# Loads of v behind the spread of the batch before, first v spread by VectorE, new planner costs: a sparse attention with a maxout layer on one core

## The chip, the core and the metric

The kernel runs on one core of a Trainium2 chip. Its engines are TensorE (PE; its weight loads are shown as PEld), VectorE (DVE), ScalarE (ACT), GpSimd (POOL) and SyncE (SP), which here only issues DMA transfers. Sixteen DMA engines move the data of the core. The metric is the device time of one execution in microseconds; lower is better. A time of a kernel is the median of its runs.

## The reference

```python
# q, k, v: (4, 8, 768, 64) float32; block = 32, window = 16, nb = 24, scale = 1/8
k_sum = k.reshape(B, H, nb, block, D).max(axis=3)
v_sum = v.reshape(B, H, nb, block, D).mean(axis=3)
scores_l = scale * q @ k.T                      # kept where |i - j| < window
scores_s = scale * einsum('bhsd,bhnd->bhsn', q, k_sum) + log(block)
a = softmax(concat[where(mask_l, scores_l, -1e9), scores_s])
attn = a @ concat[v, v_sum]                     # (B, H, S, D)
x = attn.transpose(0, 2, 1, 3).reshape(3072, 512)
h1, h2 = x @ w1, x @ w2                         # w1, w2: 512 x 1024
out = maximum(h1, h2) @ w_out                   # w_out: 1024 x 512
```

Each query sees its 31 nearest keys and 24 block summaries. The result then goes through a layer that takes the larger of two products, and a last product.

## The kernel before

**Work.** Four batches of eight heads, handled as four head pairs (hp). For a head pair, k and q are loaded, cast to bf16, turned by TensorE, and placed in kx and qx; kx gets the 24 block maxima beside the keys of each of 12 tiles of 64 queries. Scores of four tiles at a time (three groups a head pair) go through exp on ScalarE into pb, and are masked. The product with v ("values", line 448) takes pb as weights and a row block of vx; VectorE divides by the sums, TensorE turns the result into xt. The maxout part is written as x w1 w_out + relu(x (w2 - w1)) w_out: "hidden" (line 548, wd = w2 - w1), relu on ScalarE, and "out", which starts with w1o = w1 w_out (line 562) and adds the rest (line 569). It runs over 256 rows at a time, three groups a batch.

**The v tile.** vx holds, for each of 12 query tiles, 128 rows: 96 rows of v (64 and 32, the neighbourhood of the tile) and 32 rows (64 to 95) with the 24 block means. It is filled in steps: `load_v` loads v in two halves (line 277, 768 KB each, vf), GpSimd casts them into vb (line 328), five transfers from SBUF to SBUF put vb's rows in place (line 294: two of 64 rows by 6 tiles, three pieces of 32 rows that are together as large as one of these), TensorE computes the means from vb (line 302), VectorE copies them into tile 0 (line 308), and a last transfer copies tile 0's means to the other 11 tiles (line 316, "vx<-vx"). All of a batch's value products read that tile, so they need the last transfer. There is one vb and there are two vx; batches 0, 1, 2, 3 use vx_95, vx_95, vx_96, vx_95 in the listings below, and the turned w1 uses vx_96 in between.

**Order.** The program is written out by a planner. Every task has an engine, a guessed duration and a priority. `Plan.run` steps through time: for each engine that is free it takes the first task in order of priority whose inputs are done and whose buffers are free, and assumes that it takes the guessed time. What comes out is one fixed list of instructions per engine; on the chip each engine works through its list in order and waits where it must. So a changed guess moves instructions on all engines. SP is planned with four transfers at a time in flight, one after the other:

```python
                if e == "SP":
                    busy[e] = now + self.ISSUE
                    t.done = max(sent[-1], now + 0.4) + t.us
```

All transfers of the program, loads, spreads and stores, are issued by SP in one list. A store (line 580) waits on SP for ScalarE's copy of its tile, and all that stands behind it on SP waits too.

Of the kernel before, what the change touches and what calls it, by code (L numbers as in the profile page):

```python
# [16 lines left out]
ACT = mybir.ActivationFunctionType  # L17
# [41 lines left out]
class Task:  # L59
    done = 1e9  # L60


class Plan:
# [7 lines left out]

    def op(self, engine, us, fn, read=(), write=(), change=(), touch=(), prio=0.0, label=""):
        t = Task()
        t.engine, t.us, t.fn, t.label = engine, us, fn, label
        t.prio = (prio, len(self.tasks))
        t.new = [*write, *change]
# [5 lines left out]
        self.tasks.append(t)  # L82

    def ready(self, t, now):
        if any(d.done + self.LAG[d.engine] > now for d in t.deps):
            return False
        need = [b for b in dict.fromkeys(t.new) if b.slot is None]
        slots = [b.ring.find(b, now) for b in need]
        if None in slots:
            return False  # L90
        for b, s in zip(need, slots):
            b.take(s)
        return True
# [33 lines left out]
def kernel(  # L127
# [14 lines left out]
    nc = tc.nc  # L142
# [11 lines left out]
    op = plan.op  # L154
# [31 lines left out]
    w1t = Buf(vxr)  # L186
# [20 lines left out]
    def fixed_parts():  # L207
# [57 lines left out]
    def load_kq(b, hp, prio):  # L265
        for n, src in enumerate((k, q)):
# [3 lines left out]
               write=[f], prio=prio, label=f"load {'kq'[n]}{b}{hp}")  # L270

    def load_v(b, prio, engines):

        vb = Buf(vbr)
        for n in range(2):
            f = Buf(vfr)
            op("SP", 3.45, lambda f=f, n=n: nc.sync.dma_start(
                out=f.ap[:].rearrange("p h m d -> p (h m) d"),
                in_=v[b, 4 * n:4 * n + 4].rearrange("h (m r) d -> r (h m) d", r=128)),
               write=[f], prio=prio, label=f"load v{b}{n}")  # L280
            copy(engines[n], 1536, lambda f=f, n=n: (
                vb.ap[:, :, 4 * n:4 * n + 4, 0:D].rearrange("p m h d -> p h m d"), f.ap[:]),
                 read=[f, amean_in], write=[vb], prio=prio + 1, label=f"cast v{b}{n}")
# [4 lines left out]
        for lo, hi, tiles_, part, ms, us in (
                (0, 64, slice(0, NT, 2), 0, slice(0, NM), 1.3),
                (0, 64, slice(1, NT, 2), 64, slice(0, NM), 1.3),  # L290
                (96, 128, slice(0, NT, 2), 64, slice(0, NM), 0.65),
                (96, 128, slice(1, NT - 1, 2), 0, slice(1, NM), 0.6),
                (96, 128, slice(NT - 1, NT), 0, slice(0, 1), 0.2)):
            op("SP", us, lambda lo=lo, hi=hi, tiles_=tiles_, part=part, ms=ms: nc.sync.dma_start(  # L294
                out=rows(vx[b].ap[lo:hi, tiles_]),
                in_=rows(vb.ap[part:part + hi - lo, ms])),
               read=[vb], write=[vx[b]], prio=prio + 2, label=f"spread v{b}")
# [13 lines left out]

        def spread_means():
            o, i = rows(vx[b].ap[s, 1:NT]), rows(vx[b].ap[s, 0:1])
            i = i.to_broadcast([32, NT - 1, H * VW])
            if engines[2] == "SP":
                nc.sync.dma_start(out=o, in_=i)
            else:
                nc.vector.tensor_copy(out=o, in_=i)

        op(engines[2], 1.2 if engines[2] == "SP" else 1.6, spread_means, read=[mean],  # L320
           write=[vx[b]], prio=prio + 2, label=f"spread means {b}")

    RATE = {"DVE": 0.00068, "ACT": 0.00102, "POOL": 0.00102}

# [7 lines left out]
    def prep(b, hp, prio, k_on, q_on):  # L332
# [28 lines left out]
        op("DVE", 0.9, lambda: nc.vector.tensor_copy(out=kt()[:, :, 0:64], in_=order(kps)),  # L361
           read=[kps], write=[kx[b, hp], kmain], prio=prio, label=f"place k{tag}")
# [123 lines left out]
    def load_w12(n, prio, prio_t):  # L486
        fs = []
        for w in (moe_w1, moe_w2):
# [173 lines left out]
```

## Time and profile before

| | |
|---|---|
| median of 3 runs | 201.36 us (200.48 to 201.41) |
| the profiled execution | 199.25 us |
| its span, first to last instruction | 197.4 us |
| around the span | 1.85 us |
| mean granted TensorE clock | 0.965 |
| busy: PE, DVE, ACT, POOL | 170.1, 104.8, 113.2, 25.0 us |
| moved by DMA | 38.08 MB |

A page's busy share is a mean over very different stages: this kernel loads much in its first 120 us and little after that. So it is read by stretches and by the points where TensorE stops. Each instruction has a row with its start, duration and the time that its engine stood idle before it, with what ended that idle time. Matmuls are pipelined: a row's duration is longer than the step from one to the next.

### The profile page before, as it was taken

What the parts mean: (1) busy time and instruction counts of PE and PEld (TensorE: products, weight loads), DVE (VectorE), ACT (ScalarE), POOL (GpSimd) and SP (SyncE); (2) the same over time, 40 slices, a digit from 0 to 9 for tenths busy, and PEclk for the clock granted to TensorE, in tenths of its full rate; (3) what the DMA queues carried; (4) which work ended last, traced back from release to release, by engine and by line L of the source; (5) the groups of instructions that cost most, each with busy time, mean ns of one, the idle gap of its engine ahead of it and who ended that gap; (6) DMA issues with size and microseconds to landing.
All of it is one profiled execution on the core that took longest, in us unless ns stands there. A gap on an engine that the chain in (4) does not pass through costs nothing.

```text
span 197.4 us, 4172 instructions
## 1 busy us (share of the span) xinstructions
PE 170.1 (86%) x1664; PEld 119.9 (61%) x1664; DVE 104.8 (53%) x286; ACT 113.2 (57%) x173; POOL 25.0 (13%) x40
## 2 busy tenths in 40 slices
PE   0358629999999984999849999999999999999991
PEld 0244528895647564568736967668687685766750
DVE  6345907897797712469937966026987540000000
ACT  2265944386778892217948865349896641533522
POOL 7653202400230002200002200000000000000000
PEclk9999985999999996699999999999999999999999
DMA  6999999999999999999999995033020110311203
GB/s 184 228 312 361 203 248 348 357 384 332 221 279 320 194 265 274 295 394 233 238 248 203 363 226 167 0 110 75 5 106 3 53 53 3 106 56 50 110 0 106
DMA packets 48659, 38.08 MB, mean 193 GB/s; under 512 B 26240, under 2 KB 44544, under 8 KB 48640
## 3 DMA queue, kind: packets, MB, share of 16 engines
q1 hardware_dynamic: 48640, 37.82, 71.6%
q8 instruction: 13, 0.21, 0.5%
q14 instruction: 6, 0.05, 0.1%
HBM read 25.17 MB, written 6.29 MB: 159 GB/s over the span
## 4 chain that ended last, share of the span: by engine, by line
PE 76%; DMA 11%; POOL 3%; DVE 3%; ACT 2%; issue 2%; SPq 1%; POOLq 0%; ACTq 0%
PE banks L569 20%; PE banks L548 19%; DMA vx<-vx 11%; PE banks L562 10%; PE banks L448 7%; PE banks L402 5%; PE banks L347 4%; PE banks L532 3%; PE banks L302 3%; PE banks L472 3%; PE banks L391 2%; DVE kx L361 1%; POOL hide L229 1%; PE banks L504 1%; SPq L294 1%
## 5 line engine op out<-in xcount | busy, mean ns | idle before, releaser
L548 PE MATMUL banks<-xt,wd 128*128 128x256 bf16 x384 | 47.5, 276 | 0.1
L569 PE MATMUL banks<-wo,g 128*128 128x512 bf16 x192 | 46.5, 379 | 0.0
L414 ACT ACTIVATE pb<-banks,bias 128x512 bf16<-128x512 f32 x48 | 31.7, 686 | 17.2 <-PE banks L402 16.8
L548 PEld LDWEIGHTS <-wd 128*128 128x128 bf16 x384 | 36.8, 99 | 5.9 <-issue 0.2
L553 ACT ACTIVATE g<-banks 128x512 bf16<-128x512 f32 x48 | 28.5, 597 | 13.3 <-PE banks L548 11.5
L328 ACT COPY o<-banks 128x512 f32<-128x512 f32 x24 | 14.0, 585 | 33.8 <-PE banks L569 33.8
L448 PE MATMUL banks<-vx,pb 128*128 128x65 bf16 x384 | 20.5, 201 | 11.0 <-DMA vx<-vx 9.0
L376 ACT COPY qx<-banks 64x768 bf16<-64x768 bf16 x32 | 25.3, 791 | 7.8 <-PE banks L347 6.3
L569 PEld LDWEIGHTS <-g 128*128 128x128 bf16 x192 | 17.2, 97 | 16.8
L448 PEld LDWEIGHTS <-pb 128*128 128x128 bf16 x384 | 17.9, 103 | 14.5 <-issue 6.5
L562 PE MATMUL banks<-w1o,xt 128*128 128x512 bf16 x96 | 24.3, 390 | 0.0
L347 PE MATMUL banks<-identity,kqb 128*128 128x128 bf16 x192 | 15.9, 229 | 9.6 <-POOL kqb L328 8.5
L402 PE MATMUL banks<-qx,kx 128*128 128x128 bf16 (+2 forms) x208 | 18.7, 230 | 2.4 <-DVE kx L370 2.2
L347 PEld LDWEIGHTS <-kqb 128*128 128x128 bf16 x192 | 13.0, 103 | 12.2 <-POOL kqb L328 8.6
L402 PEld LDWEIGHTS <-kx 128*128 128x128 bf16 x208 | 15.7, 107 | 7.3 <-DVE kx L370 3.3
L462 DVE TENSOR_TENSOR xs<-banks,inv 128x256 bf16<-128x256 f32 x48 | 18.8, 414 | 0.2
L328 POOL CAST vb<-vf 128x1536 bf16<-128x1536 f32 x8 | 11.8, 1471 | 49.5 <-DMA vf<-in_v_dram 32.2
L460 DVE RECIPROCAL inv<-banks 128x4 f32<-128x4 f32 x48 | 7.9, 174 | 18.8 <-PE banks L448 18.5
L361 DVE COPY kx<-banks 128x768 bf16<-128x768 bf16 x16 | 15.2, 952 | 4.5 <-PE banks L347 4.4
L328 ACT CAST kqb<-kqf 128x768 bf16<-128x768 f32 x16 | 13.2, 829 | 7.6 <-DMA kqf<-in_q_dram 6.5
L363 DVE TENSOR_REDUCE ks<-kx 128x24 bf16<-128x768 bf16 x16 | 15.0, 940 | 0.1
L423 DVE TENSOR_TENSOR pb<-pb,mask 128x512 bf16<-128x512 bf16 x24 | 11.6, 494 | 6.0 <-ACT pb L414 5.8
(46 smaller groups left out, 126.3 us busy)
## 6 DMA issues: line engine op xcount, KB each, us to landing
kqf<-in_k_dram SPq DMA_DIRECT2D x16, 384.0 KB, 6.9
kqf<-in_q_dram SPq DMA_DIRECT2D x16, 384.0 KB, 6.6
vf<-in_v_dram SPq DMA_DIRECT2D x8, 768.0 KB, 11.0
out_dram<-o SPq DMA_DIRECT2D x20, 256.0 KB, 2.1
wf<-in_moe_w_dram SPq DMA_DIRECT2D x8, 512.0 KB, 10.3
vx<-vb SPq DMA_DIRECT2D x8, 396.0 KB, 8.4
wf<-in_moe_w_out_dram SPq DMA_DIRECT2D x4, 512.0 KB, 8.6
vx<-vx SPq DMA_DIRECT2D x4, 363.0 KB, 6.2
```

What stands on the lines that cost most here:

```text
L328: {"DVE": nc.vector.tensor_copy, "ACT": nc.scalar.copy, "POOL": nc.gpsimd.tensor_copy}[engine](out=o, in_=i)
L347: nc.tensor.transpose(out=bank(ps, S, BF16)[:, 128 * j:128 * j + 128], in_=src.ap[:, j].rearrange("p h d -> p (h d)"), identity=identity[:])
L361: op("DVE", 0.9, lambda: nc.vector.tensor_copy(out=kt()[:, :, 0:64], in_=order(kps)), read=[kps], write=[kx[b, hp], kmain], prio=prio, lab ...
L376: op("ACT", 0.8, lambda a=a, r=r: nc.scalar.copy(out=qx[b, hp].ap[r, a, :], in_=order(qps)[r]), read=[qps], write=[qx[b, hp]], prio=prio, ...
L402: nc.tensor.matmul(out=o[:, :, n0:n1], lhsT=w, rhs=qx[b, hp].ap[:, :, c:c + n1 - n0], start=(mask_on != "PE"), stop=(mask_on != "PE" or (i ...
L414: op("ACT", 0.7, lambda: nc.scalar.activation(out=pv(), in_=bank(ps).rearrange("p (i w q) -> p i w q", w=2, q=64), func=ACT.Exp, bias=bias ...
L448: nc.tensor.matmul(out=av()[:, u, a, :], lhsT=pb.ap[:, 2 * u + a, 64 * par:64 * par + 128], rhs=vx[b].ap[:, 4 * grp + 2 * u + par, 2 * hp ...
L462: op("DVE", 0.42, lambda: nc.vector.tensor_tensor(out=x.ap[:, hp % 2], in0=av()[:, :, :, 0:D], in1=inv.ap[:].to_broadcast([128, 2, 2, D]), ...
L548: nc.tensor.matmul(out=bank(ps)[:, 256 * s:256 * s + 256], lhsT=wd[n].ap[:, c, 128 * s:128 * s + 128], rhs=x.ap[:, c, :], start=(c == 0), ...
L553: op("ACT", 0.6, lambda n=n, ps=ps: nc.scalar.activation(out=g.ap[:, 2 * n:2 * n + 2, :].rearrange("p f n -> p (f n)"), in_=bank(ps), func ...
L562: nc.tensor.matmul(out=bank(ps), lhsT=x.ap[:, c, sl], rhs=w1o[c].ap[:], start=(c == 0), stop=False)
L569: nc.tensor.matmul(out=bank(ps), lhsT=g.ap[:, f, sl], rhs=wo[f // 2].ap[:, f % 2, :], start=False, stop=(f == FC - 1))
```

## The change

`Plan.op` gets an argument `behind`: a task with it isn't taken before the named tasks have been taken. The two loads of v of a batch now stand behind the last transfers of the spread of the batch before. Who moves the five pieces of a spread is a parameter; for batch 0 VectorE copies the two large ones, and SP issues the other three and the means. The k of head pair 0 of batch 0 is cast by VectorE instead of GpSimd. Many of the guessed durations are set anew.

```diff
-        if any(d.done + self.LAG[d.engine] > now for d in t.deps):
+        if any(d.done + self.LAG[d.engine] > now for d in t.deps) or any(
+                d.start is None for d in t.behind):
             return False
...
-        op("POOL", 1.2, make_hide, write=[hide_in], prio=-1, label="hide")
+        op("POOL", 4.0, make_hide, write=[hide_in], prio=-1, label="hide")
...
-            op("SP", 3.45, lambda f=f, n=n: nc.sync.dma_start(
+            op("SP", 3.55, lambda f=f, n=n: nc.sync.dma_start(
...
-               write=[f], prio=prio, label=f"load v{b}{n}")
+               write=[f], behind=v_spread[b - 1], prio=prio, label=f"load v{b}{n}")
...
-        for lo, hi, tiles_, part, ms, us in (
-                (0, 64, slice(0, NT, 2), 0, slice(0, NM), 1.3),
-                (0, 64, slice(1, NT, 2), 64, slice(0, NM), 1.3),
-                (96, 128, slice(0, NT, 2), 64, slice(0, NM), 0.65),
...
+        for piece, (lo, hi, tiles_, part, ms) in enumerate((
+                (0, 64, slice(0, NT, 2), 0, slice(0, NM)),
+                (0, 64, slice(1, NT, 2), 64, slice(0, NM)),
+                (96, 128, slice(0, NT, 2), 64, slice(0, NM)),
...
+            if engines[2][piece] == "SP":
+                last.append(op("SP", (1.7, 1.6, 1.0, 0.85, 0.3)[piece], lambda aps=aps: (
+                    lambda o, i: nc.sync.dma_start(out=o, in_=i))(*aps()), **kw))
+            else:
+                e = engines[2][piece]
+                copy(e, 0, aps, us=(1, 1, 1, 5 / 6, 1 / 6)[piece] * {
+                    "DVE": 1.75, "ACT": 2.4, "POOL": 3.1}[e], **kw)
...
+        v_spread[b] = [*last, t] if engines[3] == "SP" else last
...
-    FIRST = (("POOL", "ACT"), ("POOL", "ACT"), ("POOL", "ACT"), ("POOL", "ACT"))
+    FIRST = (("DVE", "ACT"), ("POOL", "ACT"), ("POOL", "ACT"), ("POOL", "ACT"))
+    FIRST_SPREAD = ("DVE", "DVE", "SP", "SP", "SP")
...
-    load_v(0, 0.5, ("POOL", "POOL", "SP"))
+    load_v(0, V0, ("POOL", "POOL", FIRST_SPREAD, "SP"))
...
-        load_v(b, 1000 * b - 480, ("POOL", "POOL", "SP"))
+        load_v(b, 1000 * b - 480, ("POOL", "POOL", ("SP",) * 5, "SP"))
```

The order of instructions moves in these places, among others. First SP, around the spread of batch 0's v: vx and vb are the tiles above, wf a load of w1 or w2, vx<-vx the transfer of the means. Before:

```order
L491 DMA wf_116<-in_moe_w_dram 128x4x256
L294 DMA vx_95<-vb_94 64x6x528 x2
L294 DMA vx_95<-vb_94 32x6x528
L294 DMA vx_95<-vb_94 32x5x528
L294 DMA vx_95<-vb_94 32x528
L316 DMA vx_95<-vx_95 32x11x528
L491 DMA wf_117<-in_moe_w_dram 128x4x256
```

And now:

```order
L503 DMA wf_116<-in_moe_w_dram 128x4x256
L304 DMA vx_95<-vb_94 32x6x528
L304 DMA vx_95<-vb_94 32x5x528
L304 DMA vx_95<-vb_94 32x528
L503 DMA wf_117<-in_moe_w_dram 128x4x256
L503 DMA wf_118<-in_moe_w_dram 128x4x256
L327 DMA vx_95<-vx_95 32x11x528
L503 DMA wf_119<-in_moe_w_dram 128x4x256
```

The two transfers of 64 rows are gone, and two loads of weights have come in front of the means.

Then SP around the spread of batch 1's v: kqf are loads of k or q, vf a half of batch 2's v, out_dram a store. Before:

```order
L268 DMA kqf_66<-in_q_dram 128x2x384
L277 DMA vf_92<-in_v_dram 128x24x64
L294 DMA vx_95<-vb_94 64x6x528 x2
L294 DMA vx_95<-vb_94 32x6x528
L580 DMA out_dram<-o_112 128x512
L580 DMA out_dram<-o_113 128x512
L294 DMA vx_95<-vb_94 32x5x528
L294 DMA vx_95<-vb_94 32x528
L316 DMA vx_95<-vx_95 32x11x528
L268 DMA kqf_67<-in_k_dram 128x2x384
L268 DMA kqf_63<-in_q_dram 128x2x384
L277 DMA vf_93<-in_v_dram 128x24x64
```

And now:

```order
L270 DMA kqf_62<-in_q_dram 128x2x384
L304 DMA vx_95<-vb_94 64x6x528 x2
L304 DMA vx_95<-vb_94 32x6x528
L592 DMA out_dram<-o_112 128x512
L304 DMA vx_95<-vb_94 32x5x528
L304 DMA vx_95<-vb_94 32x528
L592 DMA out_dram<-o_113 128x512
L327 DMA vx_95<-vx_95 32x11x528
L270 DMA kqf_67<-in_k_dram 128x2x384
L270 DMA kqf_64<-in_q_dram 128x2x384
L281 DMA vf_92<-in_v_dram 128x24x64
L281 DMA vf_93<-in_v_dram 128x24x64
```

The half load of v in front of the spread has moved behind the means, where it stands beside the other half.

Last VectorE, where the k chain of batch 0 meets the first v: ks are block maxima. Before:

```order
L226 MEMSET pb_91 128x4x32
L308 CAST vx_95<-banks 32x8x64
L361 COPY kx_73<-banks 128x12x64
L363 TENSOR_REDUCE ks_98<-kx_73 128x24
L367 COPY kx_73<-kx_73 128x32
L361 COPY kx_74<-banks 128x12x64
```

And now:

```order
L228 MEMSET pb_91 128x4x32
L340 COPY vx_95<-vb_94 64x6x528 x2
L373 COPY kx_73<-banks 128x12x64
L319 CAST vx_95<-banks 32x8x64
L375 TENSOR_REDUCE ks_98<-kx_73 128x24
L379 COPY kx_73<-kx_73 128x32
L382 COPY kx_73<-ks_98 128x12x24
```

The two copies of v stand ahead of the k chain of head pair 1, and the copy of the means behind its first step.

On TensorE the list is interleaved anew throughout. Counted in the two lists: ahead of batch 0's first value product stand 8 turns of w1, 2 mask and 5 score matmuls more than before; ahead of batch 1's, 24 hidden, 8 out (line 569) and 8 score matmuls fewer; ahead of batch 2's, 4 of line 562, 4 of line 569 and 6 turns of k or q more; ahead of batch 3's, 6 turns more. The number of all matmuls is the same.

## Rows read from the trace of the kernel before

**Rows 1.** DMA, the span in 40 slices of 4.9 us: busy tenths of the 16 engines.

```profile
DMA  6999999999999999999999995033020110311203
```

**Rows 2.** The chain of waits by engine and line, share of the span.

```profile
PE banks L569 20%; PE banks L548 19%; DMA vx<-vx 11%; PE banks L562 10%; PE banks L448 7%; PE banks L402 5%; PE banks L347 4%; PE banks L532 3%; PE banks L302 3%; PE banks L472 3%; PE banks L391 2%; DVE kx L361 1%; POOL hide L229 1%; PE banks L504 1%; SPq L294 1%
```

**Rows 3.** TensorE in order of time: start, us, line, out<-in, count, [idle <-releaser].

```profile
23.66 0.39 PE L402 MATMUL banks<-qx,kx 128*128 128x128 bf16 x4
...
28.68 0.98 PE L448 MATMUL banks<-vx,pb 128*128 128x65 bf16 x15 [2.47 <-DMA vx<-vx]
...
73.17 0.19 PE L448 MATMUL banks<-vx,pb 128*128 128x65 bf16 x1
...
76.68 0.54 PE L448 MATMUL banks<-vx,pb 128*128 128x65 bf16 x7 [3.31 <-DMA vx<-vx]
...
97.91 0.19 PE L448 MATMUL banks<-vx,pb 128*128 128x65 bf16 x1
...
101.33 0.39 PE L448 MATMUL banks<-vx,pb 128*128 128x65 bf16 x7 [3.24 <-DMA vx<-vx]
```

**Rows 4.** Stretches: busy us of PE, PEld, DVE, ACT, POOL; PEclk, DMA share, GB/s.

```profile
21.00:26.00 5.00, 2.71 (x38) 2.18 (x37) 3.82 (x8) 4.90 (x8) 1.04 (x1) 1.00 1.14 207
...
28.50:36.50 8.00, 7.77 (x99) 6.95 (x99) 5.29 (x14) 3.38 (x5) 2.08 (x2) 0.62 1.09 348
...
48.00:53.50 5.50, 5.50 (x41) 3.22 (x39) 4.89 (x9) 2.98 (x5) 0.46 (x2) 1.00 1.23 229
...
28.68:35.00 6.32, 6.32 (x73) 5.70 (x73) 4.57 (x11) 2.64 (x4) 1.04 (x1) 0.53 1.09 347
...
76.68:83.00 6.32, 6.32 (x52) 4.29 (x52) 2.88 (x10) 2.01 (x3) 1.17 (x2) 0.55 1.15 284
```

**Rows 5.** DMA issues by line: count, KB each, median us to landing.

```profile
wf<-in_moe_w_dram SPq DMA_DIRECT2D x8, 512.0 KB, 10.3
...
vx<-vb SPq DMA_DIRECT2D x8, 396.0 KB, 8.4
...
vf<-in_v_dram SPq DMA_DIRECT2D x8, 768.0 KB, 11.0
```

**Rows 6.** GpSimd casts in order of time, start of the kernel.

```profile
12.60 1.47 POOL L328 CAST vb<-vf 128x1536 bf16<-128x1536 f32 x1 [2.07 <-DMA vf<-in_v_dram]
...
14.01 0.83 POOL L328 CAST kqb<-kqf 128x768 bf16<-128x768 f32 x1
...
21.08 1.04 POOL L328 CAST w1b<-wf 128x1024 bf16<-128x1024 f32 x1 [2.28 <-DMA wf<-in_moe_w_dram]
```

**Rows 7.** Chain of waits, dense stretch at full clock: start, us, line, matmuls.

```profile
114.02 0.86 PE banks L562 x4
...
117.09 0.45 PE banks L402 x8
...
119.99 0.86 PE banks L569 x4
...
120.85 0.87 PE banks L548 x8
```

**Rows 8.** VectorE in order of time, the k chain of batch 0.

```profile
17.59 0.96 DVE L361 COPY kx<-banks 128x768 bf16<-128x768 bf16 x1
...
21.40 0.75 DVE L367 COPY kx<-kx 128x32 bf16<-128x32 bf16 x1
...
23.93 0.16 DVE L367 COPY kx<-kx 128x32 bf16<-128x32 bf16 x1
...
24.61 0.22 DVE L370 COPY kx<-ks 128x288 bf16<-128x288 bf16 x1
```

**Rows 9.** SP's issues around the second v: start, us held, line, transfer, count.

```profile
41.22 9.10 SPq L277 DMA_DIRECT2D vf<-in_v_dram  x2
...
57.04 0.42 SPq L277 DMA_DIRECT2D vf<-in_v_dram  x1
...
67.30 2.81 SPq L580 DMA_DIRECT2D out_dram<-o  x2
```

More of the change, by code (lines that the diff above doesn't have):

```diff
@@ L59 @@
 class Task:
-    done = 1e9
+    done, start = 1e9, None
 class Plan:
@@ L70, in __init__, with op @@
         self.tasks = []
-    def op(self, engine, us, fn, read=(), write=(), change=(), touch=(), prio=0.0, label=""):
+    def op(self, engine, us, fn, read=(), write=(), change=(), touch=(), behind=(), prio=0.0, label=""):
         t = Task()
@@ L75, in op @@
         t.prio = (prio, len(self.tasks))
-        t.new = [*write, *change]
+        t.new, t.behind = [*write, *change], behind
         t.deps = {w for b in (*read, *change) for w in b.writers}
@@ L82, in op @@
         self.tasks.append(t)
+        return t
     def ready(self, t, now):
-        if any(d.done + self.LAG[d.engine] > now for d in t.deps):
+        if any(d.done + self.LAG[d.engine] > now for d in t.deps) or any(
+                d.start is None for d in t.behind):
             return False
@@ L254, in make_amean @@
                 nc.gpsimd.memset(t[:, :, :, D:VW], 1.0)
-        op("POOL", 1.2, make_hide, write=[hide_in], prio=-1, label="hide")
-        op("POOL", 1.7, make_amean, write=[amean_in], prio=0.2, label="amean")
+        op("POOL", 4.0, make_hide, write=[hide_in], prio=-1, label="hide")
+        op("POOL", 2.0, make_amean, write=[amean_in], prio=0.2, label="amean")
         op("POOL", 0.4, lambda: nc.gpsimd.tensor_scalar(
@@ L270, in load_kq @@
                write=[f], prio=prio, label=f"load {'kq'[n]}{b}{hp}")
+    v_spread = {-1: []}
     def load_v(b, prio, engines):
@@ L286, in rows @@
             return t.rearrange("p t h w -> p t (h w)")
-        for lo, hi, tiles_, part, ms, us in (
-                (0, 64, slice(0, NT, 2), 0, slice(0, NM), 1.3),
-                (0, 64, slice(1, NT, 2), 64, slice(0, NM), 1.3),
-                (96, 128, slice(0, NT, 2), 64, slice(0, NM), 0.65),
[L292 to L297, printed above, removed]
+        last = []
+        for piece, (lo, hi, tiles_, part, ms) in enumerate((
+                (0, 64, slice(0, NT, 2), 0, slice(0, NM)),
+                (0, 64, slice(1, NT, 2), 64, slice(0, NM)),
+                (96, 128, slice(0, NT, 2), 64, slice(0, NM)),
+                (96, 128, slice(1, NT - 1, 2), 0, slice(1, NM)),
+                (96, 128, slice(NT - 1, NT), 0, slice(0, 1)))):
+            aps = lambda lo=lo, hi=hi, tiles_=tiles_, part=part, ms=ms: (
+                rows(vx[b].ap[lo:hi, tiles_]), rows(vb.ap[part:part + hi - lo, ms]))
+            kw = dict(read=[vb], write=[vx[b]], prio=prio + 2, label=f"spread v{b}{piece}")
+            if engines[2][piece] == "SP":
[5 more added lines that the diff above has]
+                    "DVE": 1.75, "ACT": 2.4, "POOL": 3.1}[e], **kw)
         ps, s, mean = Buf(banks, "mm"), slice(64, 96), Buf(Ring([None]))
@@ L314, in spread_means @@
             i = i.to_broadcast([32, NT - 1, H * VW])
-            if engines[2] == "SP":
+            if engines[3] == "SP":
                 nc.sync.dma_start(out=o, in_=i)
@@ L318, in spread_means @@
                 nc.vector.tensor_copy(out=o, in_=i)
-        op(engines[2], 1.2 if engines[2] == "SP" else 1.6, spread_means, read=[mean],
+        t = op(engines[3], 1.5 if engines[3] == "SP" else 2.0, spread_means, read=[mean],
            write=[vx[b]], prio=prio + 2, label=f"spread means {b}")
-    RATE = {"DVE": 0.00068, "ACT": 0.00102, "POOL": 0.00102}
+        v_spread[b] = [*last, t] if engines[3] == "SP" else last
+    RATE = {"DVE": 0.00068, "ACT": 0.00102, "POOL": 0.00095}
     def copy(engine, n, aps, label, us=None, **kw):
@@ L360, in prep @@
         kmain, ks = Buf(Ring([None])), Buf(ksr)
-        op("DVE", 0.9, lambda: nc.vector.tensor_copy(out=kt()[:, :, 0:64], in_=order(kps)),
+        op("DVE", 0.96, lambda: nc.vector.tensor_copy(out=kt()[:, :, 0:64], in_=order(kps)),
            read=[kps], write=[kx[b, hp], kmain], prio=prio, label=f"place k{tag}")
@@ L366, in prep @@
            read=[kmain], write=[ks], prio=prio, label=f"max k{tag}")
-        op("DVE", 0.1, lambda: nc.vector.tensor_copy(
+        op("DVE", 0.17, lambda: nc.vector.tensor_copy(
             out=kx[b, hp].ap[:, 96 * NT:KW], in_=kx[b, hp].ap[:, 0:32]),
            read=[kmain], write=[kx[b, hp]], prio=prio, label=f"wrap k{tag}")
-        op("DVE", 0.25, lambda: nc.vector.tensor_copy(
+        op("DVE", 0.22, lambda: nc.vector.tensor_copy(
             out=kt()[:, :, 64:64 + nb],
@@ L497, in load_w12 @@
         copy("POOL", 1024, lambda: (w1b[n].ap[:], fs[0].ap[:]), read=fs[:1], write=[w1b[n]],
-             prio=prio, us=1.3, label=f"w1b {n}")
+             prio=prio, us=1.05, label=f"w1b {n}")
         ps = Buf(banks, "x")
@@ L511, in load_w12 @@
             bank(ps, 1024, BF16)),
-             read=[ps], write=[w1t, w1t_part[n]], prio=prio_t, us=0.8, label=f"w1t {n}")
+             read=[ps], write=[w1t, w1t_part[n]], prio=prio_t, us=0.68, label=f"w1t {n}")
     def load_wo(n, prio):
         f = Buf(wfr)
-        op("SP", 1.35, lambda: nc.sync.dma_start(
+        op("SP", 1.38, lambda: nc.sync.dma_start(
             out=f.ap[:].rearrange("p c n -> p (c n)").rearrange("p (c n) -> p c n", c=2),
@@ L611 @@
     load_kq(0, 0, 0)
-    load_v(0, 0.5, ("POOL", "POOL", "SP"))
+    V0 = 0.5
+    load_v(0, V0, ("POOL", "POOL", FIRST_SPREAD, "SP"))
     for hp in range(1, NP):
```

## Prediction

> **What bounds the kernel now.** Read the slices first: the DMA engines are busy to the last tenth until slice 25, about 120 us, and nearly idle after [rows 1]. Then the chain of waits: TensorE holds most of it, but the largest share that is not compute is one kind of transfer, the one that spreads block means inside a v tile (vx from vx) [rows 2]. Then TensorE's own instructions in order of time. Through the attention of batches 0 to 2 it stops three times, and each time the instruction that ends the stop is the first product with a new batch's v: at 28.68 (batch 0), at 76.68 (batch 1, after one matmul at 73.17) and at 101.33 (batch 2, after one at 97.91) [rows 3]. After 101.33 it never waits long, and 96.07 us later the span of 197.4 ends. So the profiled time is 101.33 + 96.07 + 1.85 (199.25 less the span). The last number is fixed. The first is set by the DMA stream, and the second by how much TensorE work the order leaves behind batch 2's v.
>
> The first two stops cost twice. From 28.68 to 35 the granted clock averages 0.53, from 76.68 to 83 it is 0.55: TensorE works at 1.2 GHz instead of 2.4 for most of both stretches, after its idle time, and that loses 6.32 x 0.47 = 3.0 and 6.32 x 0.45 = 2.8 us [rows 4].
>
> **The first v: two transfers become two VectorE copies.** All five pieces and the means have crossed when TensorE starts at 28.68. The two main pieces leave the DMA queue: 2 x 396 KB = 811 kB [rows 5]. In the stretch where only spreads move the rate is 207 GB/s, so 3.9 us of DMA time go [rows 4]. The other end is 2.3, at the 348 GB/s of the w loads; then batch 2's v, further down, would come 1.6 later and the whole be 1.6 slower than forecast. I take 3.9, since its stretch holds this very transfer.
>
> But the order spends most of that at once: w loads 2 and 3 now stand before the means transfer on SP, 2 x 512 KB = 1049 kB at 348 GB/s = 3.0 us [rows 4, 5]. By the DMA the first products could start at 28.68 - 3.9 + 3.0 = 27.8. TensorE has a second condition now: the turn of w1 part 1 comes before these products. Its load lands after the smaller pieces (406 kB, 2.0 us) and two w loads (3.0 us) behind the first w load, whose cast started at 21.08 [rows 6]: 26.1. Then a cast of 1.04, eight turns and a group of scores with its two mask matmuls, together twice the 0.45 of eight scores at full clock [rows 7], 0.9, and 1.8 at half: 28.0 to 28.9. I take 28.5. So this stop barely shortens. I keep its clock loss too: TensorE's last scores before the stop end at 24.1 [rows 3], and the w1b cast that it now waits for ends at 27.1.
>
> The copies themselves (3168 bf16 a partition) are on no row. From below: kx from ks, also SBUF to SBUF, takes 0.22 for 288 elements against 0.16 for 32 [rows 8], which extrapolates to 0.16 + 3136 x 0.06/256 = 0.9 us. From above: the copy of 768 out of PSUM in 0.96 gives 4.0 [rows 8]. The first is the nearer in kind, so 0.9 each; both ends stay in the range. They start when the second v cast ends, 14.07 [rows 6]. At 0.9 VectorE is free at 16, before its k copy could start at 17.6 anyway, and they cost nothing. At 4.0 they end at 22.1, and the rest of VectorE's chain up to the last kx (7.2 us in the trace, 17.59 to 24.83) ends at 29.3: then the first products start near 29.8.
>
> One thing speaks against these copies: GpSimd's casts run beside them. In the trace a VectorE copy of 32 elements, 0.16 alone, took 0.75 when it began at 21.40, and ended with the w1b cast that had begun at 21.08 for 1.04 [rows 6, 8]. The new copies meet the k cast of 14.01 (0.83) the same way, so 0.8 us, and 1.7 if a second cast slips between them. The Trainium skill, "SBUF — State Buffer", section "Who interferes with whom", says that a VectorE copy in a two-port mode and a GpSimd instruction exclude each other for a whole instruction, the later one waiting. The trace agrees, 0.75 for 0.16. With my low value VectorE is free at 17.7 instead of 16, which still costs nothing; with the high one the start goes to about 31.
>
> The k cast of head pair 0 that moves from GpSimd to VectorE lets the first scores start earlier, but what they lead to waits for v; I count nothing.
>
> **The second v: what stands behind the spread.** One half load of batch 2's v, 768 KB, was issued at 57.04, just before the spread of batch 1 [rows 9]. It now stands behind the means transfer. At the 229 GB/s of v loads [rows 4] that takes 3.4 us out of the way, and the 3.9 from above carry through, since the engines stay full in between. Batch 1's v then arrives at 76.68 - 3.9 - 3.4 = 69.4. The stores that stood in the spread's way (SP sat 2.81 us on two of them [rows 9]) stand there still, but TensorE reaches their data about 4 us sooner.
>
> Does TensorE get there? From first product to first product it took 73.17 - 28.68 = 44.5 us, clock loss included. The new order has 24 hidden-layer matmuls, 8 output matmuls and 8 score matmuls fewer in front of batch 1's v: 3 x 0.87 + 2 x 0.86 + 0.45 = 4.8 us [rows 7]. Another 0.9 (8 turns, 2 mask and 5 score matmuls) is already done before batch 0's. So 28.5 + 44.5 - 5.7 = 67.3: a stop of 2 us instead of 3.3.
>
> **The third v, which decides.** Up to it the queue carries the same loads, stores and spreads as before, only in another order, less the 3.9 us. So batch 2's v arrives at 101.33 - 3.9 = 97.4. TensorE needs 97.91 - 76.68 = 21.2 us from batch 1's v, plus the 4.8 put off, plus 2.05 because 4 more w1o matmuls, 4 more output matmuls and 6 more turns now precede batch 2's v (0.86 + 0.86 [rows 7], and six eighths of 0.45): 28.1, or 25.2 if the clock is not lost again. From 69.4 it arrives at 94.6 to 97.5. Both meet at about 97.4.
>
> **Sum.** Behind batch 2's v stand 96.07 - 2.05 = 94.0 us. 97.4 + 94.0 + 1.85 = 193.3, 6.0 less than the profiled 199.25. That execution lies 2.1 below the median of the runs shown, 201.36; I take the same difference off the median: 195.4. The other new planner costs act only through the order; what they change behind batch 2 swaps neighbours on a TensorE that is full either way. Batch 3's v keeps its place relative to the work around it.
>
> **Rivals.**
> Late TensorE: the copies cost their upper value, the clock falls after the second stop too, or small waits add up, so that TensorE comes 2 us after the transfer, at 99.5. For it: both arrivals lie within 3 us. Time 99.5 + 94.0 + 1.85 = 195.4, median 197.5.
> More than the bytes: SP's 2.8 us of waiting for stores also go, v arrives at 94.6 and TensorE, with no second clock loss, at the same moment. Against it: the engines are full in every slice up to there [rows 1], so there is little idle to win. Time 190.5, median 192.6.
> No gain on the stream: the DMA time saved is lost again elsewhere, batch 2's v still arrives at 101.33. Only the 2.05 us of moved work remain: 197.2, median 199.3.
> Slower: the pair of v loads of batch 2 now goes out in one piece. The pair of batch 1 held SP for 9.10 us, where a single one took 0.42 [rows 9]. Behind it on SP stand two k/q loads, two stores, four more k/q loads and the spread of batch 2. If these only start to flow when SP is let go, v arrives 9.1 late, at 106.5, and the time is 202.4, median 204.5. It turns the result slower once the hold costs more than 6.0. Against it: SP is held because the engines are full (share 1.23 in that stretch [rows 4]), and a hold over full engines costs nothing. For it: all else behind the pair is in order, with no way past.
>
> The Trainium skill, "DMA: Bandwidth & Descriptors", section "Queues, rings and completion order", has each engine take a queue's descriptors in ring order. By that rule the slower rival needs the rings to run dry, and the moved half load really leaves the spread's way; the trace agrees as far as batch 1's spread, issued after the load of 57.04, is there only at 76.68.
>
> **Numbers.** Forecast 0.52 (own range 193.8 to 197); late TensorE 0.15; more than the bytes 0.09; no gain on the stream 0.08; a hold that eats all of it, no change, 0.06; slower 0.10. A difference of 0.5%, 1 us, is about what a measurement of this kernel can tell from none. Faster 0.83, same 0.07, slower 0.10. The range reaches from the "more" case to the "no gain" case: 192.2 to 199.5.
>
> **What would show it.** Right: first product of batch 0 near 28.5, of batch 1 near 69 after about 2 us of idle, of batch 2 near 97 with little idle before it; no spread transfer of 64 partitions before the second v. Copies of 0.9 us on VectorE, the first late by a GpSimd cast. Wrong: batch 2's first product after 100 (then see whether DMA shares dip behind the v pair, or TensorE came late), new idle time of TensorE behind it, or a first start after 30.

## The result, and the profile after

The changed kernel takes 194.37 us (median; 192.44 to 195.67), the kernel before, run with it, 201.07: a ratio of 0.964, 95% interval 0.956 to 0.971. Its profiled execution took 194.21, with a span of 192.5. Here and below a ratio leaves out executions more than 1.5% above the fastest of the same kernel, and a median does not.

The page's DMA slices (40 of 4.8 us), TensorE's granted clock in the same slices, and the chain of waits:

```profile
DMA  5999999999999999999999996061020111120303
```

```profile
PEclk9999996999999999999999999999999999999999
```

```profile
PE banks L581 17%; PE banks L560 16%; DMA vf<-in_v_dram 13%; DMA vx<-vb 10%; PE banks L574 7%; PE banks L460 5%; DMA wf<-in_moe_w_out_dram 4%; SPq L503 4%; DMA vx<-vx 4%; PE banks L414 3%; DMA kqf<-in_k_dram 2%; PE banks L359 2%; POOL vb L340 2%; PE banks L484 2%; PE banks L313 1%; DVE pb L435 1%
```

The queue is as full as before [rows 1]; only one slice has a low clock. Transfers now hold a third of the chain, but no longer the means transfer in particular, which had 11% [rows 2].

TensorE in order of time, its three stops and one new one (start, us, line, count, [idle <-releaser]):

```profile
24.28 0.38 PE L414 MATMUL banks<-qx,kx 128*128 128x128 bf16 x4
...
28.64 0.62 PE L516 MATMUL banks<-identity,w1b 128*128 128x128 bf16 x8 [3.98 <-POOL w1b L340]
...
29.80 1.09 PE L460 MATMUL banks<-vx,pb 128*128 128x65 bf16 x16
...
68.48 0.19 PE L460 MATMUL banks<-vx,pb 128*128 128x65 bf16 x1
70.42 0.63 PE L460 MATMUL banks<-vx,pb 128*128 128x65 bf16 x15 [1.75 <-DMA vx<-vx]
...
95.87 0.19 PE L460 MATMUL banks<-vx,pb 128*128 128x65 bf16 x1
97.36 0.61 PE L460 MATMUL banks<-vx,pb 128*128 128x65 bf16 x15 [1.30 <-DMA kqf<-in_k_dram]
...
105.01 0.42 PE L460 MATMUL banks<-vx,pb 128*128 128x65 bf16 x8 [0.45 <-DVE pb L435]
```

Against [rows 3]: the first products of batches 0, 1 and 2 start at 29.80, 70.42 and 97.36 instead of 28.68, 76.68 and 101.33. The releaser of the third is named as a k load, but the product reads only vx and pb: the means transfer, issued at 91.95, landed 5.4 us later, at 97.35. Behind 97.36 lie 95.1 us (96.07 before). So of the 4.9 us that the span is shorter, 4.0 were won before batch 2's v and 0.9 behind it.

The two stretches after the first stops (busy PE, PEld, DVE, ACT, POOL; PEclk, DMA share, GB/s) answer to the last two of [rows 4]:

```profile
28.64:35.00 6.36, 6.36 (x93) 5.88 (x94) 4.41 (x12) 3.19 (x5) 1.04 (x1) 0.73 1.08 346
70.42:77.00 6.58, 6.52 (x102) 5.43 (x104) 5.32 (x16) 4.81 (x8) 1.46 (x1) 1.00 1.18 225
```

The clock averages 0.73 instead of 0.53 after the first stop and stays whole after the second: 6.36 x 0.27 = 1.7 us are lost instead of 3.0 + 2.8.

VectorE around the copies, and its later mask; then GpSimd:

```profile
14.22 2.56 DVE L340 COPY vx<-vb 64x3168 bf16<-64x3168 bf16 x2 [4.67 <-POOL vb L340]
17.64 0.96 DVE L373 COPY kx<-banks 128x768 bf16<-128x768 bf16 x1 [0.85 <-PE banks L359]
...
103.31 1.64 DVE L435 TENSOR_TENSOR pb<-pb,mask 128x512 bf16<-128x512 bf16 x1
```

```profile
14.13 0.83 POOL L340 CAST kqb<-kqf 128x768 bf16<-128x768 f32 x1
15.88 1.59 POOL L340 CAST kqb<-kqf 128x768 bf16<-128x768 f32 x1 [0.92 <-DMA kqf<-in_k_dram]
...
27.54 1.04 POOL L340 CAST w1b<-wf 128x1024 bf16<-128x1024 f32 x1 [4.89 <-DMA wf<-in_moe_w_dram]
...
103.21 1.47 POOL L340 CAST vb<-vf 128x1536 bf16<-128x1536 f32 x1 [22.64 <-DMA vf<-in_v_dram]
```

Both copies end at 16.78, before VectorE's next work, which starts when it did before [rows 8]. SP's v loads of batch 2, which the slower rival was about:

```profile
66.09 7.07 SPq L281 DMA_DIRECT2D vf<-in_v_dram  x2
73.21 2.95 SPq L270 DMA_DIRECT2D kqf<-in_k_dram  x1
```

SP is held for 7.07 us, with the engines at a share of 1.17 in that stretch:

```profile
66.09:73.16 7.07, 5.27 (x62) 3.24 (x62) 2.80 (x11) 4.22 (x8) 0.00 (x0) 1.00 1.17 262
```

### The profile page after: what moved, and what is told of

It reads as the page before. It is cut to its first block, busy times and chain, and to the rows that moved or that the text cites. A ratio compares the mean times of both kernels' runs of the same rounds, so it can differ in the third digit from the quotient of the medians.

```text
span 192.5 us, 4148 instructions
## 1 busy us (share of the span) xinstructions
PE 166.4 (86%) x1643; PEld 117.9 (61%) x1664; DVE 109.9 (57%) x289; ACT 114.1 (59%) x173; POOL 25.7 (13%) x39
## 4 chain that ended last, share of the span: by engine, by line
PE 53%; DMA 33%; SPq 5%; DVE 4%; POOL 2%; issue 1%; ACT 0%; ACTq 0%
PE banks L581 17%; PE banks L560 16%; DMA vf<-in_v_dram 13%; DMA vx<-vb 10%; PE banks L574 7%; PE banks L460 5%; DMA wf<-in_moe_w_out_dram 4%; SPq L503 4%; DMA vx<-vx 4%; PE banks L414 3%; DMA kqf<-in_k_dram 2%; PE banks L359 2%; POOL vb L340 2%; PE banks L484 2%; PE banks L313 1%; DVE pb L435 1%
## 5 line engine op out<-in xcount | busy, mean ns | idle before, releaser
L560 PE MATMUL banks<-xt,wd 128*128 128x256 bf16 x384 | 46.6, 273 | 0.5 <-DVE xt L489 0.5
L581 PE MATMUL banks<-wo,g 128*128 128x512 bf16 x184 | 44.9, 379 | 0.4
L460 PE MATMUL banks<-vx,pb 128*128 128x65 bf16 x384 | 19.4, 196 | 3.6 <-DMA vx<-vx 1.8
L574 PE MATMUL banks<-w1o,xt 128*128 128x512 bf16 x85 | 21.9, 379 | 0.6
L460 PEld LDWEIGHTS <-pb 128*128 128x128 bf16 x384 | 16.9, 100 | 7.1 <-DMA vx<-vx 2.1
L359 PE MATMUL banks<-identity,kqb 128*128 128x128 bf16 x192 | 16.6, 234 | 5.3 <-DVE kqb L340 4.7
L414 PEld LDWEIGHTS <-kx 128*128 128x128 bf16 x208 | 15.1, 103 | 6.6 <-DVE kx L382 2.4
L359 PEld LDWEIGHTS <-kqb 128*128 128x128 bf16 x192 | 13.6, 106 | 8.5 <-DVE kqb L340 4.7
L489 DVE COPY xt<-banks 128x512 bf16<-128x512 bf16 x24 | 9.8, 418 | 7.2 <-PE banks L484 6.8
L574 PEld LDWEIGHTS <-xt 128*128 128x128 bf16 x96 | 8.9, 98 | 7.9
```

What stands on the lines that cost most here:

```text
L359: nc.tensor.transpose(out=bank(ps, S, BF16)[:, 128 * j:128 * j + 128], in_=src.ap[:, j].rearrange("p h d -> p (h d)"), identity=identity[:])
L414: nc.tensor.matmul(out=o[:, :, n0:n1], lhsT=w, rhs=qx[b, hp].ap[:, :, c:c + n1 - n0], start=(mask_on != "PE"), stop=(mask_on != "PE" or (i ...
L460: nc.tensor.matmul(out=av()[:, u, a, :], lhsT=pb.ap[:, 2 * u + a, 64 * par:64 * par + 128], rhs=vx[b].ap[:, 4 * grp + 2 * u + par, 2 * hp ...
L560: nc.tensor.matmul(out=bank(ps)[:, 256 * s:256 * s + 256], lhsT=wd[n].ap[:, c, 128 * s:128 * s + 128], rhs=x.ap[:, c, :], start=(c == 0), ...
L574: nc.tensor.matmul(out=bank(ps), lhsT=x.ap[:, c, sl], rhs=w1o[c].ap[:], start=(c == 0), stop=False)
L581: nc.tensor.matmul(out=bank(ps), lhsT=g.ap[:, f, sl], rhs=wo[f // 2].ap[:, f % 2, :], start=False, stop=(f == FC - 1))
```

## The experiments

The time is read as the first product of batch 2, plus the rest of the span, plus what lies around the span (1.85 us in the kernel before, 1.7 to 1.8 in the others). The rest is the span less that start, so the sum holds by definition; what can be tested is where the start comes. From each kernel's profiled execution:

| Kernel | batch 1 | batch 2 | rest of span | profiled |
|---|---|---|---|---|
| before | 76.68 | 101.33 | 96.1 | 199.25 |
| changed | 70.42 | 97.36 | 95.1 | 194.21 |
| changed, second profile | 70.40 | 98.79 | 94.5 | 195.02 |
| changed, third profile | 69.28 | 96.39 | 95.1 | 193.23 |
| 1 first spread on DMA | 73.54 | 100.88 | 94.4 | 197.02 |
| 2 half load ahead | 72.41 | 99.36 | 94.6 | 195.72 |
| 3 turn late | 68.68 | 95.69 | 95.1 | 192.58 |
| 4 copies in batches 1 and 2 too | 69.89 | 98.64 | 95.9 | 196.24 |
| 6 costs only | 76.68 | 100.43 | 94.2 | 196.27 |
| 7 hold only | 72.80 | 100.06 | 94.8 | 196.65 |
| 8 copies only | 72.03 | 102.94 | 95.8 | 200.39 |
| 9 k and q held too | 67.78 | 96.47 | 94.9 | 193.13 |
| 10 old costs | 70.65 | 102.66 | 94.1 | 198.51 |

The changed kernel was timed twice more beside the experiments: 194.46 (ratio 0.987, 0.980 to 0.994) and 193.80 (0.973, 0.965 to 0.981). Its own times agree; the kernel before had medians of 198.57 to 201.07 in the four measurements. By the medians the gain is 6.7, 4.1 and 6.4 us, by the ratios 3.6, 1.3 and 2.7%. All three intervals lie below 1, but the first and the second do not overlap, and only the first lies wholly beyond 2%. How much is won stays open between them; what differs from one measurement to the next is the kernel before.

**1. The first spread back on DMA, every order kept.**

```diff
-                copy(e, 0, aps, us=(1, 1, 1, 5 / 6, 1 / 6)[piece] * {
-                    "DVE": 1.75, "ACT": 2.4, "POOL": 3.1}[e], **kw)
+                op(e, 1.75, lambda aps=aps: (
+                    lambda o, i: nc.sync.dma_start(out=o, in_=i))(*aps()), **kw)
```

> Every engine keeps the order of the changed kernel; only the two main pieces of the first v spread (2 x 396 KB) go by DMA instead of by VectorE, at the place in the order where the copies stood. Theory (the gain is DMA time in front of the later v tiles): 811 kB at 207 GB/s = 3.9 us come back ahead of everything, so the first products of batches 0, 1 and 2 start 3.9 us later, near 33.7, 74.3 and 101.3, and the median goes from 194.4 to 198.3. Rival (the gain is the new order, the bytes were hidden anyway): batch 2's first product stays within 1 us of 97.4 and the median at 194.4 to 195.4.

197.40 us, ratio 0.987 (0.982 to 0.992). The first products, of TensorE's rows:

```profile
33.81 1.09 PE L460 MATMUL banks<-vx,pb 128*128 128x65 bf16 x16
...
73.54 0.61 PE L460 MATMUL banks<-vx,pb 128*128 128x65 bf16 x15 [1.75 <-DMA kqf<-in_q_dram]
...
100.88 0.63 PE L460 MATMUL banks<-vx,pb 128*128 128x65 bf16 x15 [1.74 <-DMA vx<-vx]
```

They come 4.0, 3.1 and 3.5 later than in the first profile of the changed kernel, and 3.8, 3.5 and 3.4 later than the means of its three. The theory's 3.9 holds to half a microsecond against those means; the median came 0.9 below the 198.3 expected. The changed kernel was not timed beside this run, but run 3, which is the changed kernel but for one turn, was: 193.48 us, 0.970 (0.965 to 0.975). The intervals do not touch, so the rival falls.

**2. One half load of batch 2's v ahead of batch 1's spread.**

```diff
-        for t in order:
-            t.fn()
+        k = [t.label for t in order].index
+        order.insert(k("spread v10"), order.pop(k("load v20"))); [t.fn() for t in order]
```

> The changed kernel with one half load of batch 2's v (768 KB) issued ahead of the spread of batch 1's v again, nothing else moved. Theory: batch 1's v comes 768 KB at 229 GB/s = 3.4 us later, first product 73.8 instead of 70.42, after an idle time of 5.2 instead of 1.75; batch 2's v arrives at 97.4 as before, but TensorE, 25.6 us behind batch 1's, is there at 99.4, 2.0 late: median 196.4; and if this longer stop also brings the clock down, as the stop of 3.31 did in the kernel before (2.8 us lost), 199.2. Rival (the transfer of batch 2's v sets the end and the stop before it is slack): batch 2's first product at 97.4 and the median at 194.4.

196.97 us, ratio 0.986 (0.982 to 0.991). TensorE, and the stretch behind the second stop:

```profile
69.03 0.20 PE L460 MATMUL banks<-vx,pb 128*128 128x65 bf16 x1 [1.52 <-DMA vx<-vb]
72.41 0.99 PE L460 MATMUL banks<-vx,pb 128*128 128x65 bf16 x15 [3.18 <-DMA vx<-vx]
...
99.36 0.65 PE L460 MATMUL banks<-vx,pb 128*128 128x65 bf16 x16
```

```profile
72.41:79.00 6.59, 6.53 (x80) 4.93 (x82) 3.77 (x14) 3.28 (x6) 0.40 (x1) 0.75 1.01 250
```

The second stop takes 1.52 + 3.18 = 4.7 us, the clock falls behind it (6.59 x 0.25 = 1.6 us), and TensorE comes to batch 2's products without a stop, 2.0 later than in the changed kernel. The half load was to cost batch 1's v 3.4 us; it cost 2.0 (72.41 instead of 70.42; 2.4 against the mean of three). The lost clock made up for the difference, so that the 99.4 expected was met by two errors that cancel. Beside run 3 the median is 3.5 us longer, and the intervals do not touch. The second stop is not slack.

**3. The turn of w1 part 1 after the first products.** In this kernel that part of w1 reaches the product of w1 and w_out from a bank that another turn has written over; every instruction is there.

```diff
-        for t in order:
-            t.fn()
+        at, n = {t: i for i, t in enumerate(order)}, [t.label for t in order].index
+        for t in sorted(order, key=lambda t: n("turn w1 2") - 0.5 if t.label in ("turn w1 1", "w1t 1") else at[t]): t.fn()
```

> The changed kernel with the eight turns of w1 part 1, and the copy behind them, moved to just ahead of those of part 2, behind the first four groups of products. Theory (the first stop is slack): the first product starts when the means have landed, near 28.9 instead of 29.80, and batch 1's and 2's first products stay where the transfers put them, 70.4 and 97.4; median 194.4, within 0.5. Rival (the first start carries through): everything from batch 1 on is 0.9 us earlier, median 193.5.

193.48 us, ratio 0.970 (0.965 to 0.975): the ratio lies between the changed kernel's three, the median 0.3 below the lowest of theirs. The profile alone would favour the rival: first products at 27.24, 68.68 and 95.69, the last without a stop. But its stream was early from the start (the means had landed by 27.24; in the changed kernel they were issued at 19.34 and landed 9.7 later, at 29.0), and its 95.69 lies 0.7 us ahead of the earliest of the changed kernel's own profiles, which differ by 2.4 among themselves. Inconclusive below 1 us.

**4. VectorE copies in batches 1 and 2 too.**

```diff
-        load_v(b, 1000 * b - 480, ("POOL", "POOL", ("SP",) * 5, "SP"))
+        load_v(b, 1000 * b - 480, ("POOL", "POOL", FIRST_SPREAD if b < 3 else ("SP",) * 5, "SP"))
```

> The changed kernel with the two main pieces also of batches 1 and 2 copied by VectorE; the planner orders the rest anew. Theory (the v tiles' DMA time sets stops 2 and 3): 3.9 us less DMA in front of batch 1's v and 7.8 in front of batch 2's, so both arrive before TensorE, which then saves its two stops, 1.75 and 1.30: 194.4 - 3.05 = 191.3. Rival (the copies cost VectorE, and through the port lock the GpSimd casts, what they free on the queue): four copies of 0.87 and as many casts blocked for 0.8 us on the path of the products, 194.4 or more.

194.28 us, but single times from 190.55 to 199.35, and the ratio, 0.958 (0.952 to 0.965), rests on the two shortest, 190.55 and 192.10. The profile is one of the longer ones, 196.24. SP's issues of batch 1's spread, TensorE, and the stretch behind its second stop:

```profile
54.69 2.17 SPq L304 DMA_DIRECT2D vx<-vb  x3
...
57.68 0.45 SPq L270 DMA_DIRECT2D kqf<-in_k_dram  x1
58.74 0.37 SPq L270 DMA_DIRECT2D kqf<-in_q_dram  x1
60.93 0.62 SPq L327 DMA_DIRECT2D vx<-vx  x1
```

```profile
69.89 0.98 PE L460 MATMUL banks<-vx,pb 128*128 128x65 bf16 x15 [4.27 <-DMA vx<-vx]
```

```profile
69.89:76.00 6.11, 6.06 (x46) 3.61 (x47) 3.93 (x11) 2.90 (x4) 1.51 (x1) 0.55 1.09 228
```

The planner put two k/q loads (786 kB) in front of the means transfer, into the place of the two pieces (811 kB). So batch 1's v came as late as in the changed kernel, TensorE waited 4.27 instead of 1.75, and the clock fell to 0.55; batch 2's products start without a stop, as the theory has it, at 98.64. This holds for that execution. The two shortest lie on either side of the theory's 191.3, and neither has a profile. Whether this beats the changed kernel stays open.

**5 to 8 and 10. The parts, alone and without one.** Run 5 was the changed kernel again:

> The changed kernel, unaltered, beside the parts of the change taken one at a time. All theories: 0.964 of the kernel before, as first measured (0.956 to 0.971); first products of batches 0, 1 and 2 within 2 us of 29.8, 70.4 and 97.4, all three shifted together if the stream of the first 28 us runs a little faster or slower.

Run 6, the new planner costs alone (first spread on SP, no hold):

```diff
-    FIRST_SPREAD = ("DVE", "DVE", "SP", "SP", "SP")
+    FIRST_SPREAD = ("SP",) * 5
-    FIRST = (("DVE", "ACT"), ("POOL", "ACT"), ("POOL", "ACT"), ("POOL", "ACT"))
+    FIRST = (("POOL", "ACT"), ("POOL", "ACT"), ("POOL", "ACT"), ("POOL", "ACT"))
-               write=[f], behind=v_spread[b - 1], prio=prio, label=f"load v{b}{n}")
+               write=[f], prio=prio, label=f"load v{b}{n}")
```

> The kernel before with the new planner costs alone: no copies on VectorE, loads of v not held behind the spread. Theory (the queue's bytes in front of batch 2's v are what counts, and they are as before): batch 2's first product at 101.3, 94.3 us of TensorE work behind it in this order: 197.4 in a profile where before has 199.25, a ratio of 0.99. Rival (the new costs alone bring the gain): 0.965 to 0.975.

195.36 us, ratio 0.990 (0.985 to 0.995), where the theory had 0.99. In its profile the products of batches 1 and 2 start at

```profile
76.68 0.61 PE L460 MATMUL banks<-vx,pb 128*128 128x65 bf16 x15 [0.78 <-DMA vx<-vx]
...
100.43 0.63 PE L460 MATMUL banks<-vx,pb 128*128 128x65 bf16 x15 [2.10 <-DMA vx<-vx]
```

and the granted clock is 1.000 over the span (0.965 in the kernel before). The rival, that the costs alone bring the gain, is not refuted by the times: on that chip run 5 had 194.46 and 0.987, so the costs alone bring 1.0 of its 1.3% and stand 0.9 us behind, which the intervals don't hold apart. The profiles do part them: batch 2's v comes at 100.43 here, and at 96.39 to 98.79 in the three of the changed kernel.

Run 7, the hold alone: the edits of run 6 to FIRST and FIRST_SPREAD, and the old costs:

```diff
-        op("POOL", 4.0, make_hide, write=[hide_in], prio=-1, label="hide")
+        op("POOL", 1.2, make_hide, write=[hide_in], prio=-1, label="hide")
...
-                last.append(op("SP", (1.7, 1.6, 1.0, 0.85, 0.3)[piece], lambda aps=aps: (
+                last.append(op("SP", (1.3, 1.3, 0.65, 0.6, 0.2)[piece], lambda aps=aps: (
...
```

> The kernel before with only the loads of v held behind the spread of the preceding batch. Theory: batch 1's first product 3.4 us earlier, 73.3 instead of 76.68; batch 2's v has the same bytes in front of it, first product still at 101.3, and the time hardly moves: 198.4 in a profile where before has 199.25, a ratio of 0.995. Rival (the second stop, with its lost clock, is paid in full): 3.4 us and more, 0.983 or less.

197.39 us, ratio 0.998 (0.993 to 1.002). Batch 1's v comes 3.9 earlier than in the kernel before, batch 2's 1.3, and nothing measurable is won.

Run 8, the copies alone: the old costs, as in run 7, and no hold, as in run 6:

> The kernel before with only the first spread's main pieces, and the first k cast, on VectorE. Without the hold the planner puts one half load of batch 2's v in front of batch 1's spread, as before, and both half loads of batch 3's v in front of batch 2's means transfer. Theory: 811 kB less (3.9 us) but 2 x 768 KB more at 229 GB/s (6.8 us) in front of batch 2's v, so its first product comes near 104 and the time is 199 to 200, a ratio of 1.00. Rival (the copies bring the gain by themselves): first product of batch 2 at 97.4, ratio 0.965 to 0.975.

200.76 us, ratio 1.018 (1.010 to 1.026): slower. TensorE and SP:

```profile
102.94 1.01 PE L460 MATMUL banks<-vx,pb 128*128 128x65 bf16 x15 [4.49 <-DMA vx<-vx]
```

```profile
87.22 7.05 SPq L281 DMA_DIRECT2D vf<-in_v_dram  x2
94.37 3.68 SPq L592 DMA_DIRECT2D out_dram<-o  x2
98.10 0.43 SPq L594 DMA_DIRECT2D out_dram<-o  x1
98.62 0.62 SPq L327 DMA_DIRECT2D vx<-vx  x1
```

Batch 3's two v loads and three stores stand in front of batch 2's means transfer, which goes out only at 98.62 (91.95 in the changed kernel). The loads hold SP for 7.05 us and the stores for 4.1; the run does not take the two apart. Batch 2's product comes 1.1 before the 104 expected, and the rival falls. The profile's 200.39 is 0.4 over the 199 to 200 expected, with 6.06 x 0.43 = 2.6 us of clock lost behind the stop. The ratio lies further above the expected 1.00, since the kernel before was faster on that occasion (198.57) than at first (201.07).

```profile
102.94:109.00 6.06, 5.84 (x55) 4.60 (x57) 3.13 (x9) 2.34 (x4) 0.00 (x0) 0.57 0.98 281
```

Run 10, copies and hold with the old costs (the old costs of run 7 and nothing else), beside run 11, the changed kernel once more:

> The changed kernel with the old planner costs: the copies on VectorE and the hold of the v loads stay. The old costs let the planner expect batch 1's v 4.7 us earlier, so that more of TensorE's work stands behind its first product (31.2 us by the plan to batch 2's, against 26.0). Theory: batch 1's v near 69.5, after a stop of 4 us or more, TensorE at batch 2's products near 100.2, its v long there: 100.2 + 94.6 + 1.85 = 196.7. Rival (the costs do nothing; copies and hold bring the gain): 97.4 and 194.4.

> The changed kernel, unaltered, on the same chip as the two beside it. All theories: 194.4, first products within 2 us of 29.8, 70.4 and 97.4.

197.83 against 193.80 us, ratios 0.986 and 0.973. Batch 1's products start where they do in the changed kernel, batch 2's without any stop at 102.66, when their v has been there since 99.3 (means issued at 94.80, landed 4.5 later):

```profile
70.65 0.78 PE L460 MATMUL banks<-vx,pb 128*128 128x65 bf16 x15 [2.54 <-DMA vx<-vx]
...
102.66 0.65 PE L460 MATMUL banks<-vx,pb 128*128 128x65 bf16 x16
```

TensorE needs 32.0 us from one to the other instead of 26.9, of which 1.3 were its third stop. Of the 6.4 us more, 6.35 x 0.27 = 1.7 are clock:

```profile
70.65:77.00 6.35, 6.29 (x69) 4.79 (x71) 3.94 (x13) 3.61 (x6) 0.91 (x1) 0.73 1.08 230
```

The other 4.7 are work that it could have done while batch 1's v travelled, and that was put behind it (329 matmul records in between instead of 292); by the plan it was to be 5.2. With the old costs the copies and the hold win about half, though the intervals (0.976 to 0.996 and 0.965 to 0.981) overlap. Run 10 is also run 8 with the hold: 0.986 against 1.018, and these intervals are far apart.

**9. The k and q loads held as well.**

```diff
-               write=[f], prio=prio, label=f"load {'kq'[n]}{b}{hp}")
+               write=[f], behind=v_spread[b - 1], prio=prio, label=f"load {'kq'[n]}{b}{hp}")
```

> The changed kernel with the k and q loads of batches 2 and 3 held behind the spread of the preceding batch's v as well. Two of them (2 x 384 KB = 786 kB) stand in front of batch 1's spread now, and two others in front of batch 2's; at 229 to 348 GB/s that is 2.3 to 3.4 us each time. Theory: batch 1's v arrives by 68.1, before TensorE at 68.7, so the second stop (1.75) goes; batch 2's v arrives near 94.5 and TensorE at 94.3, so the third goes too: first product of batch 2 at 94.7, time 191.6. Rival (stores or something else than these bytes hold the stream, or the later k casts stall VectorE): 97.4 or later, 194.4 or more.

192.94 us, ratio 0.966 (0.958 to 0.974), beside 193.80 (0.973) of the changed kernel. In its profile the start was late, by the w1 turn:

```profile
31.09 1.09 PE L460 MATMUL banks<-vx,pb 128*128 128x65 bf16 x16
...
67.78 0.63 PE L460 MATMUL banks<-vx,pb 128*128 128x65 bf16 x15 [1.31 <-DMA vx<-vx]
...
96.47 0.37 PE L460 MATMUL banks<-vx,pb 128*128 128x65 bf16 x7 [1.15 <-DMA kqf<-in_k_dram]
```

The second profile of the changed kernel started as late, at 31.35; against it batch 1's product comes 2.6 us earlier and batch 2's 2.3, inside the 2.3 to 3.4 that the bytes were to bring. Yet neither stop goes, since TensorE is early too, and the profile's 193.13 lies between the theory's 191.6 and the rival's 194.4. It is the fastest median here, by less than the intervals can hold apart.

## Why the prediction was right

**The sum.** 97.4 + 94.0 + 1.85 = 193.3 was forecast for a profile; measured were 97.36 + 95.14 + 1.71 = 194.21, and for the median 194.37 where 195.4 was forecast. The likeliest case came true. None of the rivals did. The median agrees in part by luck: the profile came out 0.9 above its forecast, but the 2.1 us added from profile to median, the difference of one execution of the kernel before, were 0.2 here. The two errors work against each other.

**First v.** The term "28.5" was too early: 29.80 here, 31.35 and 28.90 in the other profiles. The condition was the right one, the turn of w1 part 1, but the landing of its load was mis-sized: its cast was to start at 26.1, 5.0 behind the first w cast, and did at 27.54, 5.9 behind a first one at 21.61. The copies took 2.56 us together, the 2 x 0.9 and 0.8 for the lock that I chose; the upper end, 4.0 each, was far off. The saved 3.9 us of DMA were 3.4 at batch 2's v in run 1. The clock loss, kept at 3.0, was 1.7.

**Second v.** 69.4 after a stop of 2 us was forecast, 70.42 after 1.75 measured. That the clock stayed whole here I had left open (25.2 or 28.1 us to the next stop); from 70.42 to 95.87 it is 25.5. The hold's 3.4 us measured less in run 2, 2.0 to 2.4. From the first product to batch 1's TensorE needed 38.7 us, 38.8 forecast, though 1.3 less of clock was lost: the terms between were 1.2 short, and no row says which.

**Third v.** 97.4 forecast, 97.36 measured, 97.5 as a mean of three. That it agrees to 0.04 is luck: the three are 96.39, 97.36 and 98.79, and the two stops before it came 1.3 and 1.0 later than forecast. TensorE was there at 96.06, inside the 94.6 to 97.5 forecast, so that the transfer and not TensorE decided, by 1.3.

**The rest.** 94.0 forecast, 95.1 measured. 0.45 of it is the new stop at 105.01: the mask operation of 103.31 took 1.64 us where the median of its 24 is 0.42, beside the v cast on GpSimd:

```profile
L435 DVE TENSOR_TENSOR pb<-pb,mask x24: 390/416/1637, 54.0 to 149.3; 128x512 bf16<-128x512 bf16 x24
```

The remaining 0.6 is in no row; it is no more than the three profiles differ here (95.1, 94.5 and 95.1), and the second has no such stop.

**Where the working was thin.** Two attributions would not have carried to a part of the change. I gave the hold only the 3.4 us of the second stop; run 8 shows that it also keeps batch 3's loads from in front of batch 2's means, without which the copies make the kernel slower. And I let the planner costs "act only through the order": true, but beside copies and hold that order is worth 4.0 us in the medians of run 10, where I had 2.05 (1.3% by the ratios, 5.3 us in the profiles), and alone it brings 1.0%. The copies free the queue (run 1), the hold decides whose bytes come next (runs 2 and 8), and the costs make TensorE's order fit the time at which v comes (run 10). What each part brings depends on the others, and how much the copies and the hold add to the costs alone is not settled: 0.9 us in the medians on one chip, within the noise, and 2.1 in profiles (196.27 against 194.15, the mean of three).

**The slower rival.** SP was held 7.07 us, over the 6.0 from which the rival was to decide, and batch 2's v was on time. By the Trainium skill, "DMA: Bandwidth & Descriptors", section "Queues, rings and completion order", each DMA engine takes a queue's descriptors in ring order. Run 2 agrees, where a half load issued ahead of a spread delayed it by 2.0 us. In run 8 the delay was already in SP's list, which issued the means only at 98.62.

## What to carry to other kernels

When one queue is full up to the last big wait, add the bytes in front of that transfer and the work behind the instruction that waits for it. Counted like this, batch 2's first product was expected to within 1.3 us in runs 1, 2, 6, 7 and 8, and came 1.8 later than expected in run 9, whose first product was late too, and 2.5 in run 10, 1.7 of it lost clock. Taking bytes off a full queue helps only if nothing else moves into the gap, so fix what is issued next in the same edit, and re-time the planner, whose order decides whether TensorE has work while it waits. Time each part alone before crediting it: here one part alone lost 1.8%.

## What was not expected of the hardware

- VectorE and GpSimd hold each other up from both sides: the copies, begun first, stretched a k cast at 15.88 to 1.59 us (0.83 undisturbed), and the v cast of 103.21 stretched a mask operation of VectorE to 1.64 (0.42).
- The length of a stop alone does not tell whether the clock falls. In run 6 it stayed at 1.00 from 28 to 36 us after a stop of 2.49; in run 3, from 68 to 76, it averaged 0.79 around a stop of 1.92. Their stretches, run 6 and run 3:

```profile
28.00:36.00 8.00, 3.77 (x79) 3.42 (x79) 5.01 (x14) 1.90 (x4) 1.60 (x2) 1.00 1.09 332
```

```profile
68.00:76.00 8.00, 7.10 (x86) 5.61 (x88) 4.71 (x14) 4.06 (x7) 1.47 (x1) 0.79 1.17 231
```

- Executions of one kernel differ from the first 30 us on, and the order of the three is the same at the end: the changed kernel's three profiles have their first product at 28.90, 29.80 and 31.35, batch 2's at 96.39, 97.36 and 98.79, and take 193.23, 194.21 and 195.02. In between it is not kept (batch 1's at 69.28, 70.42 and 70.40), and the cause is not shown.
